# Reordering the opening attention of a fused attention and expert-mixture kernel: four scores in a row on two PSUM tiles, and a rearranged chunk 0

## The chip, the cores and the metric

The kernel runs on one core of one Trainium2 chip. The metric is device time in microseconds (us) of one execution; lower is better. The kernel before had a median of 497.34 us in its first 3 runs (496.2 to 497.48).

Names: PE is the matmul engine (TensorE), DVE the vector engine, ACT the scalar engine, POOL is GpSimd. PSUM is the memory that PE's results go to, cut in banks. Idle matmuls are matmuls of zeros whose results are not used. "The span" is the profiled execution, about 1.7 us shorter than its device time.

## The reference, cut to what matters

```python
# attention: batch 8, heads 8, sequence 576, head dimension 64
k_p = k.reshape(B, H, 72, 8, D).mean(axis=3)      # keys and values pooled by 8: 72 of each
v_p = v.reshape(B, H, 72, 8, D).mean(axis=3)
attn = softmax(q @ k_p.T / sqrt(D))               # (cut: written out in the original)
x = (attn @ v_p) reshaped to (4608 tokens, 512)
# four experts, every token through all of them
p = domain_probs / (domain_probs.sum(-1, keepdims=True) + 1e-9)
for e in range(4):
    out += p[:, e:e+1] * (maximum(x @ w1[e], 0) @ w2[e])     # w1: 512x1024, w2: 1024x512
```

## The kernel before

The kernel works in 9 chunks of 512 tokens: one for each batch's first 512 tokens, and a last one of the eight remainders. Three stages matter here.

1. **Batch 0's attention** (until about 25 us). Nothing else can fill PE yet. It runs pooling matmuls for keys and values, two groups of four heads by two halves of tokens = four "scores" (each 8 matmuls, then one exp on ACT), four contexts (one for each 128 tokens; matmuls, then a divide on DVE), a turn (transpose on PE, then a copy) of each context, and first-layer matmuls on 128 tokens at a time with the early half of w1 of expert 0.
2. **Chunk 0** (to about 69 us). The rest of the four experts for batch 0, with batch 1's attention woven in, as keys, values and weights land by DMA.
3. **The steady loop** (to the end). Both layers are multiplied as 2x2 blocks with seven products instead of eight, so sums of blocks (of x, of the weights, of the hidden layer) are formed on DVE first. The attention of the next batches is woven in; x of batch 2 and later is transposed by DMA.

The opening, as the kernel before has it (cuts are marked):

```python
    def two_banks(b):
        return att_first[turn_of("att", 2)] if b < 2 else att   # the two 2-bank tiles in turn

    def sum_keys(g):
        copies = (nc.vector.tensor_copy, nc.scalar.copy)
        for copy, (hs, kp) in zip(copies, sum_pool("kraw", g), strict=True):
            copy(out=kp_all[0:SP, hs], in_=kp.unsqueeze(2).to_broadcast([SP, 2, 2, D]))

    def context_half(r, g):
        # ... cut: x_tok is allocated ...
        c_ps = two_banks(0)                     # a whole 2-bank tile for half a context
        # ... cut: 4 matmuls, then divide() on DVE

    def scores_first(group, tok):
        # ... cut ...
        sc_ps = two_banks(0)[:].rearrange("p a (h n) -> p a h n", n=P)
        # ... cut: 8 matmuls, then one exp of 72x1024 on ACT

    def attention_first():
        # ... cut: queries, idle matmuls ...
        sum_keys(0)
        idle(1)
        keys(0, lo)
        sum_keys(1)
        scores_first(0, 0)
        keys(0, hi)
        sum_values(0)
        scores_first(1, 0)
        context_half(0, 0)
        sum_values(1)
        turn_half(0, 0)
        idle(1, chains[0][:])
        context_half(0, 1)
        scores_first(0, 1)
        idle(1, chains[1][:])
        turn_half(0, 1)
        context(0, 1)
        up_first(range(0, 4), first)
        turn(0, 1)
        scores_first(1, 1)                      # the fourth score, after first-layer work
        idle(1)
        up_first(range(0, 4), second)
        context(0, 2)
        context(0, 3)
        up_first(range(4, FCH), first)          # from here on the late half of w1
        turn(0, 2)
        up_first(range(4, 6), second)
        turn(0, 3)
        up_first(range(6, FCH), second)
        up(0, 0, range(FCH), half)
```

In chunk 0 the touched part is:

```python
        sums[1][3]()
        fold_keys(1, every)                     # DVE: adds up batch 1's keys, once they landed
        for i in range(3):
            up(0, 3, (i,))
            down(0, 0, 4 + i)
        queries(1, 0)
        # ... cut: queries, up(0, 3, ...), keys(1), scores(1, 0..2) ...
        fold_values(1, every)
        # ... cut: loads for batch 2 ...
        down_plain(0, 1, 0)
        scores(1, 3)
        down_plain(0, 1, 1)
        context(1, 0)
        # ... cut
```

```python
        POOLED = (4,)
        # ... cut
                down(*below_of[t2], i2, t2 % 2, POOLED)
```

The softmax here doesn't subtract the row's maximum and nothing guards it: scores larger than these inputs give would overflow.

## Time and profile before

| | kernel before |
|---|---|
| device time, median (range) of the first 3 runs | 497.34 us (496.2 to 497.48) |
| PE busy | 98% of the span, at a clock of 0.999 |
| first pooled-key matmul ("first key sum") | 7.92 us |
| expert 1's first 512-column first-layer matmul | 24.89 us |
| first matmul of the steady loop | 69.07 us |

The last three marks are read from the timeline. The document uses lengths made of them: **A**, from the first key sum to expert 1's first layer (16.97 us); **B**, from there to the steady loop (44.18); **C**, from there to the end of the span (425.1). A and B are what the change touches.

From the page of the kernel before: its span, busy times by engine, and the shares of the chain that ended last.

```profile
span 494.2 us, 11449 instructions
...
PE 486.7 (98%) x4656; PEld 405.9 (82%) x4663; DVE 375.9 (76%) x755; ACT 302.9 (61%) x562; POOL 115.8 (23%) x114
...
PE 98%; DVE 1%; issue 0%; DVEq 0%
```

PE is the limit, and the chain is PE almost without a break. A saved microsecond of PE waiting in A or B should therefore show at the end, if nothing later takes it back.

From the timeline of the kernel before, from 0 to 26 us. Columns: start, duration, engine, line, operation, output<-input by the program's names, shapes, count; in brackets the idle time before and what ended it.

```profile
1.26 5.20 PE L323 MATMUL unit<-H 128*128 128x512 bf16 x14 [1.26 <-DVE H L812]
...
7.92 0.69 PE L302 MATMUL unit<-wt_bf,S 64*72 64x128 bf16 x18
...
10.59 1.02 ACT L509 ACTIVATE expT<-att_first 72x1024 bf16<-72x1024 f32 x1
...
12.03 1.02 ACT L509 ACTIVATE expT<-att 72x1024 bf16<-72x1024 f32 x1 [0.42 <-PE att L505]
...
14.37 1.02 ACT L509 ACTIVATE expT<-att_first 72x1024 bf16<-72x1024 f32 x1 [0.85 <-PE att_first L505]
...
15.19 0.78 PE L592 MATMUL unit<-xT,w_bf 128*128 128x128 bf16 x8
...
16.70 0.40 PE L505 MATMUL att_first<-qT,kpT 64*128 64x128 bf16 x8
...
17.14 1.02 ACT L509 ACTIVATE expT<-att_first 72x1024 bf16<-72x1024 f32 x1 [0.31 <-PE att_first L505]
...
24.89 1.03 PE L577 MATMUL o_ps<-xT,w_bf 128*128 128x512 bf16 x3
```

The first line is the opening run of idle matmuls, the second the first key sum. The four ACT lines are the four exps. They start 2.67, 4.11, 6.45 and 9.22 us after the first key sum, though each takes only 1.02 us; three of them ended an idle spell of ACT that waited for PE's scores. The line at 16.70 is the fourth score, between first-layer matmuls that began at 15.19.

From the timeline of the kernel before, PE only, from 66 to 72 us, the first matmul of the steady loop:

```profile
69.07 0.60 PE L650 MATMUL unit<-xT,w_bf 128*128 128x256 bf16 x4
```

From the view of waits of the kernel before, PE only. Columns: who waited (engine, tile, line), for whom, us in total, times, longest.

```profile
PE unit L323 <- DVE kp L311: 0.5, 1, 0.5
PE o_ps L293 <- DVE kp L311: 0.4, 1, 0.4
PE o_ps L416 <- DVE x_tok L389: 0.3, 2, 0.2
PE att_first L401 <- DVE vp L316: 0.2, 1, 0.2
```

PE waits for the pooled keys (kp), the divided context (x_tok) and the pooled values (vp).

From the timeline of the kernel before, from 117 to 124 us, three of the sums on batch 2's x, and POOL's accumulating add:

```profile
120.91 0.43 DVE L238 TENSOR_TENSOR xs<-xs,xT 128x512 bf16<-128x512 bf16 x1 [0.89 <-DMA xT<-x_tok]
...
121.25 0.42 DVE L238 TENSOR_TENSOR xT<-xT 128x512 bf16<-128x512 bf16 x1
...
121.59 0.42 DVE L238 TENSOR_TENSOR xs<-xT,xs 128x512 bf16<-128x512 bf16 x1
121.75 1.40 POOL L732 TENSOR_TENSOR acc<-acc,addend 128x512 f32<-128x512 f32 x1
```

DVE waited for x to land by DMA, then ran its sums in 0.42 us each; POOL's add was issued 0.16 us after the last of them began.

### The profile page before, as it was taken

The numbers are of one execution on the slowest core, as the hardware profiler recorded it, in microseconds if no ns is written. First come the engines' busy times: TensorE is split into PE (matmuls) and PEld (weight loads), VectorE is DVE, ScalarE is ACT, GpSimd is POOL, SyncE is SP. The second block draws the span as 40 slices with busy tenths as digits, with TensorE's granted clock in tenths as the row PEclk, the third lists the DMA queues.
The fourth block names the chain that finished last, engine by engine and source line by source line (L and its number), as shares of the span: only waits on it lengthen the run. The fifth ranks groups of instructions, "written<-read, shape, count | busy, mean of one in ns | idle before, by whom it ended". The sixth has DMA issues, their size and how long they took to land.

```text
span 494.2 us, 11449 instructions
## 1 busy us (share of the span) xinstructions
PE 486.7 (98%) x4656; PEld 405.9 (82%) x4663; DVE 375.9 (76%) x755; ACT 302.9 (61%) x562; POOL 115.8 (23%) x114
## 2 busy tenths in 40 slices
PE   8999999999999999999999999999999999999996
PEld 4746468888889888888898889888888888888885
DVE  5495889799768975798669876796678766876674
ACT  4666536865775568656765676557655566556650
POOL 8320413233342154114421362111000100011010
PEclk9999999999999999999999999999999999999999
DMA  9999996997879669453975397320211010003003
GB/s 199 208 204 203 207 161 114 107 70 95 100 103 59 90 66 142 47 78 40 164 63 78 37 144 75 54 47 31 68 23 23 21 65 1 13 23 86 1 1 85
DMA packets 101811, 41.95 MB, mean 85 GB/s; under 512 B 73840, under 2 KB 100208, under 8 KB 101760
## 3 DMA queue, kind: packets, MB, share of 16 engines
q0 software_dynamic: 56928, 22.42, 40.8%
q1 hardware_dynamic: 43728, 17.77, 18.2%
q10 hardware_dynamic: 1104, 1.05, 0.6%
q8 instruction: 36, 0.59, 0.5%
q14 instruction: 15, 0.12, 0.1%
HBM read 45.69 MB, written 9.44 MB: 112 GB/s over the span
## 4 chain that ended last, share of the span: by engine, by line
PE 98%; DVE 1%; issue 0%; DVEq 0%
PE o_ps L718 41%; PE unit L650 40%; PE unit L577 4%; PE o_ps L744 3%; PE att L373 2%; PE att L425 2%; PE unit L323 1%; PE unit L776 1%; PE o_ps L577 1%; PE unit L592 0%; PE unit L302 0%; PE att L479 0%; PE att L462 0%; PE att_first L443 0%; PE o_ps L592 0%
## 5 line engine op out<-in xcount | busy, mean ns | idle before, releaser
L793 DVE SCALAR_TENSOR_TENSOR acc<-o_ps,p_all,acc 128x256 f32<-128x256 f32 (+1 forms) x285 | 127.2, 487 | 52.0 <-PE o_ps L718 34.6
L718 PEld LDWEIGHTS <-H 128*128 128x128 bf16 x1320 | 129.1, 98 | 16.2 <-issue 0.2
L650 PEld LDWEIGHTS <-w_bf 128*128 128x128 bf16 x1024 | 97.7, 98 | 15.1 <-issue 3.6
L631 DVE CUSTOM_DVE_ANT_0 H<-unit,partial 128x512 bf16<-128x512 f32 x128 | 87.5, 686 | 25.5 <-PE unit L650 20.9
L718 PE MATMUL o_ps<-w_bf,H 128*128 128x256 bf16 x792 | 102.6, 273 | 0.0
L650 PE MATMUL unit<-xT,w_bf 128*128 128x256 bf16 x672 | 96.4, 273 | 0.0
L665 ACT COPY partial<-unit 128x512 f32<-128x512 f32 x128 | 72.0, 590 | 33.2 <-PE unit L650 33.0
L732 POOL TENSOR_TENSOR acc<-acc,addend 128x512 f32<-128x512 f32 x24 | 30.5, 1271 | 253.7 <-ACT addend L730 197.8
L650 PEld LDWEIGHTS <-wu_bf 128*128 128x128 bf16 x768 | 73.3, 98 | 10.0 <-issue 1.5
L650 PE MATMUL unit<-xs,wu_bf 128*128 128x256 bf16 x512 | 76.9, 273 | 0.0
L718 PE MATMUL o_ps<-wt_bf,H 128*128 128x256 bf16 x528 | 68.4, 273 | 0.0
L718 PEld LDWEIGHTS <-S 128*128 128x128 bf16 x528 | 51.7, 98 | 6.4
L671 ACT ACTIVATE H<-unit 128x512 bf16<-128x512 f32 x64 | 38.2, 597 | 29.5 <-PE unit L650 29.3
L667 ACT ACTIVATE H<-unit 128x512 bf16<-128x512 f32 x64 | 38.8, 607 | 27.8 <-PE unit L650 27.8
L663 ACT COPY unit<-unit 128x512 f32<-128x512 f32 x64 | 37.4, 584 | 15.4 <-PE unit L650 15.4
L650 PE MATMUL unit<-xs,w_bf 128*128 128x256 bf16 x256 | 38.5, 273 | 0.0
L791 ACT ACTIVATE acc<-o_ps,p_all 128x256 f32<-128x256 f32 x72 | 30.2, 471 | 11.2 <-PE o_ps L718 9.9
L147 POOL DMA_DIRECT2D vraw<-in_v_dram x20 | 29.0, 1448 | 26.3 <-DMA vraw<-in_v_dram 19.8
L147 POOL DMA_DIRECT2D kraw<-in_k_dram x20 | 25.9, 1294 | 37.8 <-DMA kraw<-in_k_dram 37.8
L718 PE MATMUL o_ps<-w_bf,S 128*128 128x256 bf16 x264 | 34.2, 273 | 0.0
L718 PE MATMUL o_ps<-wt_bf,S 128*128 128x256 bf16 x264 | 34.2, 273 | 0.0
L650 PE MATMUL unit<-xT,wu_bf 128*128 128x256 bf16 x224 | 33.6, 272 | 0.0
(150 smaller groups left out, 514.3 us busy)
## 6 DMA issues: line engine op xcount, KB each, us to landing
out_dram<-acc SPq DMA_DIRECT2D x32, 256.0 KB, 4.2
w_bf<-in_moe_w_dram POOLq DMA_DIRECT2D x7, 1024.0 KB, 23.7
q_sb<-in_q_dram POOLq DMA_DIRECT2D x7, 512.0 KB, 9.7
vraw<-in_v_dram POOLq DMA_DIRECT2D x22, 144.0 KB, 6.7
kraw<-in_k_dram POOLq DMA_DIRECT2D x21, 144.0 KB, 5.5
w_bf<-in_moe_w_dram POOLq DMA_DIRECT2D x2, 512.0 KB, 8.1
wt_bf<-in_k_dram POOLq DMA_DIRECT2D x4, 144.0 KB, 5.5
wt_bf<-in_v_dram POOLq DMA_DIRECT2D x4, 144.0 KB, 4.2
```

Source lines behind the costliest of these rows:

```text
L147: nc.gpsimd.dma_start(out=raw[:], in_=rows_of(src, b, 2 * part, 2 * part + 2), accum_op=ALU.add if part else ALU.bypass)
L577: nc.tensor.matmul(out_ps, lhsT=w1_bf[:, e, kc, fc * P:(fc + 1) * P], rhs=xT[:, kc, at], start=(kc == 0), stop=(kc == KC - 1), skip_group_ ...
L631: nc.vector._custom_dve(TENSOR_ADD_SAT, out=dst, in0=ps, in1=part, s0=LARGEST, s1=0.0)
L650: nc.tensor.matmul(ps[:, n * HN:(n + 1) * HN], lhsT=lhs[:, kc, f:f + P], rhs=rhs[:, kc, :], start=(not grows and n == 0 and kc == 0), stop ...
L663: nc.scalar.copy(out=units[unit][1][:], in_=ps)
L665: nc.scalar.copy(out=part[:, step - 2], in_=ps)
L667: nc.scalar.activation(out=quarter(0, 0), in_=ps, func=ACT.Relu)
L671: nc.scalar.activation(out=quarter(0, 1), in_=ps, func=ACT.Relu)
L718: nc.tensor.matmul(ps[:, j], lhsT=lhs[:, i, j * P:(j + 1) * P], rhs=rhs[:, i, :], start=(not grows and i == 0 and j == 0), stop=(i == HF - 1),
L732: nc.gpsimd.tensor_add(out=dst, in0=dst, in1=addend[:])
L791: nc.scalar.activation(out=dst, in_=o_ps, func=ACT.Copy, scale=prob)
L793: nc.vector.scalar_tensor_tensor(out=dst, in0=o_ps, scalar=prob, in1=dst, op0=ALU.mult, op1=ALU.add,)
```

## The change

Its intent: let ACT run the four exps without gaps, so that everything behind the last one (contexts 2 and 3, their turns, the last first-layer blocks) is no longer held up. For this, the scores alternate between two 2-bank tiles, and the first context in two halves goes to the single banks that the second layer will use later. The order behind it changes: all first-layer work on the early half of w1, for all four token blocks, comes before any on the late half. Chunk 0 is reordered so that batch 1's keys and scores start earlier among other work, and the loads of expert 1's w2 and batch 1's values trade places.

The diff also moves some copies between DVE and ACT (of pooled keys and values, of the turn of context 1, and of batch 1's keys and queries).

The core of the diff (long parts cut):

```diff
-    def context_half(r, g):
+    def context_half(r, g, bank):
-        c_ps = two_banks(0)
+        c_ps = bank.rearrange("p (a n) -> p a n", a=1)
 # ... cut: scores_first, sum_keys, sum_values, turn_half and context also take their bank
-        sum_keys(0)
-        idle(1)
+        work, (B2, A2) = units[1], att_first
+        sum_keys(0, work)
+        idle(1, A2[:, 0])
+        sum_keys(1, [B2[:, 0], B2[:, 1]])
         keys(0, lo)
-        sum_keys(1)
-        scores_first(0, 0)
+        scores_first(0, 0, A2)
         keys(0, hi)
-        # ... cut: the old order, shown above
+        sum_values(0, work)
+        scores_first(1, 0, B2)
+        context_half(0, 0, chains[1][:])
+        scores_first(0, 1, A2)
+        sum_values(1, work)
+        turn_half(0, 0, chains[1][:])
+        scores_first(1, 1, B2)
+        context_half(0, 1, chains[0][:])
+        context(0, 1, A2)
+        idle(2, chains[1][:])
+        turn_half(0, 1, chains[0][:])
+        context(0, 2, B2)
+        idle(1, chains[1][:])
+        up_first(range(0, 2), first)
+        turn(0, 1)
+        up_first(range(2, 4), first)
+        context(0, 3, A2)
+        turn(0, 2)
+        up_first(range(0, 4), second)
+        turn(0, 3)
+        up_first(range(0, 4), third)
+        up_first(range(0, 4), fourth)
+        up_first(range(4, FCH), first)
+        up_first(range(4, FCH), second)
+        up(0, 0, range(4, FCH), half)
 # ... cut: chunk 0
         sums[1][3]()
-        fold_keys(1, every)
-        for i in range(3):
-            up(0, 3, (i,))
-            down(0, 0, 4 + i)
+        fold_keys(1)
+        up(0, 3, (0, 1))
+        down(0, 0, 4)
+        up(0, 3, (2, 3))
         queries(1, 0)
         queries(1, 1)
+        down(0, 0, 5)
+        keys(1, every)
 # ... cut: down(0, 0, ...) later, scores(1, ...) earlier, value fold in parts
 # ... cut: loads
         load_q(1)
+        load_w2(1)
         load_whole(1, v, "vraw")
-        load_w2(1)
```

More of the change, by code (lines that the diff above doesn't have):

```diff
@@ L257, in one_bank, with folds @@
         return spare_bank() if b == 0 else two_banks(b)[:, 0]
-    def fold(raw, hs):
-        nc.vector.tensor_add(out=raw[:, hs, 0:4, :], in0=raw[:, hs, 0:4, :],
-                             in1=raw[:, hs, 4:8, :])
-        nc.vector.tensor_add(out=raw[:, hs, 0:2, :], in0=raw[:, hs, 0:2, :],
-                             in1=raw[:, hs, 2:4, :])
+    def folds(raw):
+        return [lambda n=n: nc.vector.tensor_add(
+            out=raw[:, :, 0:n, :], in0=raw[:, :, 0:n, :], in1=raw[:, :, n:2 * n, :]) for n in (4, 2)]
     def fold_wide(what, part):
@@ L274, in fold_wide, with fold_keys @@
             nc.vector.tensor_add(out=raw[:], in0=raw[:], in1=a)
-    def fold_keys(b, hs):
+    def fold_keys(b):
         raw = raw_k if b >= BUSY else raws[("kraw", b)]
         if b < BUSY:
-            fold(raw, hs)
+            for do in folds(raw):
+                do()
         for dup in range(2):
-            nc.vector.tensor_add(out=kp_all[0:SP, hs, dup, :], in0=raw[:, hs, 0, :],
-                                 in1=raw[:, hs, 1, :])
+            nc.vector.tensor_add(out=kp_all[0:SP, :, dup, :], in0=raw[:, :, 0, :], in1=raw[:, :, 1, :])
     def keys(b, hs):
@@ L293, in keys, with sum_pool @@
             nc.tensor.transpose(kpt_ps[:, h, :], kp_all[0:SP, h], ident[:SP, :SP])
-        nc.vector.tensor_copy(out=state[("kpT", b)][:, hs, 0:SP], in_=kpt_ps[:, hs])
-    def sum_pool(nm, g):
+        copy = nc.scalar.copy if b else nc.vector.tensor_copy
+        copy(out=state[("kpT", b)][:, hs, 0:SP], in_=kpt_ps[:, hs])
+    def sum_pool(nm, g, banks):
         n = 2 * D
-        banks = [work_bank()[0:SP, 0:n] for _ in range(2)]
+        banks = [bank[0:SP, 0:n] for bank in banks]
         for r in range(ROWS):
@@ L306, in sum_pool, with sum_keys, sum_values @@
             yield slice(h, h + 2), banks[half].rearrange("j (h d) -> j h d", d=D)
-    def sum_keys(g):
-        copies = (nc.vector.tensor_copy, nc.scalar.copy)
-        for copy, (hs, kp) in zip(copies, sum_pool("kraw", g), strict=True):
+    def sum_keys(g, banks):
+        copies = (nc.scalar.copy if g else nc.vector.tensor_copy, nc.scalar.copy)
+        for copy, (hs, kp) in zip(copies, sum_pool("kraw", g, banks), strict=True):
             copy(out=kp_all[0:SP, hs], in_=kp.unsqueeze(2).to_broadcast([SP, 2, 2, D]))
-    def sum_values(g):
-        copies = (nc.vector.tensor_copy, nc.scalar.copy if g else nc.vector.tensor_copy)
-        for copy, (hs, vp) in zip(copies, sum_pool("vraw", g), strict=True):
-            copy(out=vps[0][:, hs, 0:D], in_=vp)
+    def sum_values(g, banks):
+        for hs, vp in sum_pool("vraw", g, banks):
+            nc.vector.tensor_copy(out=vps[0][:, hs, 0:D], in_=vp)
     def idle(n, w_ps=None):
@@ L325, in open_bank, with values_folds @@
     def open_bank(ps):
-        nc.tensor.matmul(ps, lhsT=ident[:], rhs=w2_bf[:, 0, 0, :], skip_group_check=True)
-    def fold_values(b, hs):
+        nc.tensor.matmul(ps, lhsT=ident[:], rhs=w1_bf[:, 0, 0, 0:NT], skip_group_check=True)
+    def values_folds(b):
         raw = raw_v if b >= BUSY else raws[("vraw", b)]
-        if b < BUSY:
-            fold(raw, hs)
-        nc.vector.tensor_add(
-            out=vps[b % 3][:, hs, 0:D], in0=raw[:, hs, 0, :], in1=raw[:, hs, 1, :]
-        )
+        return (folds(raw) if b < BUSY else []) + [lambda: nc.vector.tensor_add(
+            out=vps[b % 3][:, :, 0:D], in0=raw[:, :, 0, :], in1=raw[:, :, 1, :])]
     def queries(b, pair=0):
@@ L355, in queries @@
                 )
-        copy = nc.scalar.copy if b == 0 and pair % 2 else nc.vector.tensor_copy
+        copy = nc.scalar.copy if pair in ((1, 3), (1, 2))[b] else nc.vector.tensor_copy
         copy(out=state[("qT", b)][:, 2 * pair:2 * pair + 2], in_=qt_ps)
@@ L405, in context_half, with turn_half @@
             )
-        divide(c_ps[:, 0:1], state[("x", 0, r)][:, g:g + 1])
-    def turn_half(r, g):
+        divide(c_ps, state[("x", 0, r)][:, g:g + 1])
+    def turn_half(r, g, bank):
         if ("xT", 0) not in state:
@@ L412, in turn_half @@
         ks = slice(g * HK, (g + 1) * HK)
-        xt_ps = chains[1 - g][:].bitcast(BF16)[:, 0:HK * P].rearrange("p (k t) -> p k t", t=P)
+        xt_ps = bank.bitcast(BF16)[:, 0:HK * P].rearrange("p (k t) -> p k t", t=P)
         for i in range(HK):
@@ L417, in turn_half, with context @@
         nc.vector.tensor_copy(out=state[("xT", 0)][:, ks, r * P:(r + 1) * P], in_=xt_ps)
-    def context(b, r):
+    def context(b, r, c_ps=None):
         expT, vp = state[("expT", b)], vps[b % 3]
         x_tok = npool.tile([P, 2, NPAIR, D], BF16, name="x_tok", bufs=4)
-        c_ps = two_banks(b)
+        if c_ps is None:
+            c_ps = two_banks(b)
         for h in range(H):
@@ L440, in turn @@
             return
-        xt_ps = (one_bank(b) if b else att_first[1][:, 0] if r == 3 else chains[0][:]).bitcast(BF16)[:, 0:KC * P].rearrange("p (k t) -> p k t", t=P)
+        xt_ps = (units[1][0][:] if b else att_first[1][:, 0] if r == 3 else chains[0][:]).bitcast(BF16)[:, 0:KC * P].rearrange("p (k t) -> p k t", t=P)
         for kc in range(KC):
             nc.tensor.transpose(xt_ps[:, kc, :], x_tok[:, kc * P:(kc + 1) * P], ident[:])
-        copy = nc.vector.tensor_copy if b == 0 and r % 2 else nc.scalar.copy
+        copy = nc.vector.tensor_copy if b == 0 and r == 3 else nc.scalar.copy
         copy(out=dst, in_=xt_ps)
@@ L491, in rem_turn, with scores_first @@
         )
-    def scores_first(group, tok):
+    def scores_first(group, tok, sc_ps):
         qT = state[("qT", 0)]
@@ L499, in scores_first @@
         hs = groups(0)[group]
-        sc_ps = two_banks(0)[:].rearrange("p a (h n) -> p a h n", n=P)
+        sc_ps = sc_ps[:].rearrange("p a (h n) -> p a h n", n=P)
         for hh in range(H // 2):
@@ L516, in attention_first @@
         lo, hi = groups(0)
-        first, second, half = slice(0, P), slice(P, 2 * P), slice(HN, NT)
+        first, second, third, fourth = (slice(r * P, (r + 1) * P) for r in range(NR))
+        half = slice(HN, NT)
         idle(14)
@@ L528, in attention_first @@
         idle(1)
-        sum_keys(0)
-        idle(1)
+        work, (B2, A2) = units[1], att_first
+        work = [work[0][:], work[1][:]]
+        sum_keys(0, work)
+        idle(1, A2[:, 0])
+        sum_keys(1, [B2[:, 0], B2[:, 1]])
         keys(0, lo)
-        sum_keys(1)
-        scores_first(0, 0)
+        scores_first(0, 0, A2)
         keys(0, hi)
-        sum_values(0)
-        scores_first(1, 0)
-        context_half(0, 0)
-        sum_values(1)
-        turn_half(0, 0)
-        idle(1, chains[0][:])
-        context_half(0, 1)
-        scores_first(0, 1)
+        sum_values(0, work)
[10 more added lines that the diff above has]
+        context(0, 2, B2)
         idle(1, chains[1][:])
-        turn_half(0, 1)
-        context(0, 1)
-        up_first(range(0, 4), first)
+        up_first(range(0, 2), first)
         turn(0, 1)
-        scores_first(1, 1)
-        idle(1)
+        up_first(range(2, 4), first)
+        context(0, 3, A2)
+        turn(0, 2)
         up_first(range(0, 4), second)
-        context(0, 2)
-        context(0, 3)
+        turn(0, 3)
+        up_first(range(0, 4), third)
+        up_first(range(0, 4), fourth)
         up_first(range(4, FCH), first)
-        turn(0, 2)
-        up_first(range(4, 6), second)
-        turn(0, 3)
-        up_first(range(6, FCH), second)
-        up(0, 0, range(FCH), half)
+        up_first(range(4, FCH), second)
+        up(0, 0, range(4, FCH), half)
     hidden = {(0, 0): H_bufs[0], (0, 1): H_bufs[1], (0, 2): H_third, (0, 3): H_bufs[0]}
@@ L737, in down, with down_plain @@
             store(c, row, cols)
-    def down_plain(c, e, r):
+    def down_plain(c, e, r, fcs=range(FCH)):
         H_sb = hidden[(c, e)]
         o_ps = chains[r % 2][:]
-        for fc in range(FCH):
+        for fc in fcs:
             lhs = H_sb[:, fc // HF, r // 2, fc % HF, (r % 2) * P:(r % 2 + 1) * P]
@@ L747, in down_plain @@
             )
-        add(o_ps, c, e, r, slice(0, DM), True)
+        if fcs.stop == FCH:
+            add(o_ps, c, e, r, slice(0, DM), True)
     room = wu_bf[:, 0, 0].rearrange("p k (i d) -> p (k i) d", d=HD)
@@ L838, in first_chunk @@
                 sums[2][i]()
-            if i == 3:
+            if i == 4:
                 open_bank(chains[1][:])
                 each(*weight_sums(0))
-            if i >= 4:
-                down(0, 0, i - 4)
-                if i in (5, 6):
-                    hidden_sums(0, 0, i - 3)
+            if i == 5:
+                down(0, 0, 0)
+                hidden_sums(0, 0, 2)
+            if i == 6:
+                down(0, 0, 1)
+                hidden_sums(0, 0, 3)
+                down(0, 0, 2)
+        down(0, 0, 3)
         sums[1][3]()
-        fold_keys(1, every)
-        for i in range(3):
-            up(0, 3, (i,))
-            down(0, 0, 4 + i)
+        fold_keys(1)
+        up(0, 3, (0, 1))
+        down(0, 0, 4)
+        up(0, 3, (2, 3))
         queries(1, 0)
         queries(1, 1)
-        up(0, 3, (3,))
+        down(0, 0, 5)
+        keys(1, every)
         queries(1, 2)
+        down(0, 0, 6)
+        scores(1, 0)
+        queries(1, 3)
+        turn_of("att", 2)
         up(0, 3, (4,))
-        queries(1, 3)
-        keys(1, every)
         each(*sums[3][0:3])
+        scores(1, 1)
         up(0, 3, (5,))
-        scores(1, 0)
+        scores(1, 2)
         up(0, 3, (6,))
-        scores(1, 1)
+        each(*weight_sums(1)[0:3])
+        scores(1, 3)
         up(0, 3, (7,))
-        scores(1, 2)
-        fold_values(1, every)
+        fold_first, *fold_rest = values_folds(1)
+        fold_first()
+        down_plain(0, 1, 0)
+        each(*fold_rest)
         load_wide(0, 0)
@@ L873, in first_chunk @@
         load_wide(1, 2)
-        each(*weight_sums(1)[0:1])
-        down_plain(0, 1, 0)
-        scores(1, 3)
-        each(*weight_sums(1)[1:2])
         down_plain(0, 1, 1)
+        down_plain(0, 1, 2, range(0, 3))
         context(1, 0)
-        down_plain(0, 1, 2)
+        down_plain(0, 1, 2, range(3, FCH))
         context(1, 1)
@@ L888, in first_chunk @@
         turn(1, 2)
-        each(*weight_sums(1)[2:3])
         down_plain(0, 2, 1)
@@ L930, in pieces_later @@
                 put(start + plan["queries"], lambda b=b: queries(b))
-                put(start + plan["keys"], lambda b=b: fold_keys(b, every))
+                put(start + plan["keys"], lambda b=b: fold_keys(b))
                 put(start + plan["keys"] + (b > BUSY), lambda b=b: keys(b, every))
-                put(start + plan["values"], lambda b=b: fold_values(b, every))
+                put(start + plan["values"], *values_folds(b))
                 put_each("scores", [lambda b=b, pair=pair: scores(b, pair) for pair in range(NPAIR)])
```

## The prediction

> **What bounds the kernel now.** TensorE. The page shows PE busy 486.7 of 494.2 us (98%), clock 0.999, and the chain that ended last is 98% PE. [...] I count issue intervals: in the timeline 128-column matmuls follow one another every 56 ns, 256-column ones every 109, 512-column ones every 216. PE is full from 66 us on (table of windows). All that the change touches lies before the steady loop (its first matmul at 69.1 us); what is saved there passes to the end one for one.
>
> **Where PE loses time there.**
> - Attention of batch 0, from the first pooled-key matmul (7.92 us) to the half-wide first layer (21.39): 13.5 us. Its matmuls need about 9.4 at their issue intervals, the idle matmuls 1.1. Some 3 us are waits: for kp, vp, x_tok, and the copy behind turn 3.
> - 21.39 to 51.4 us: none (group starts match the sums of intervals to 0.1).
> - 51.4 to 68.9 us: about 0.4, 0.1 at each score group.
>
> **What the change does.** PE work is nearly unchanged: the order of instructions shows 16 more matmuls, since half of the 256-column first-layer ones become 128-column ones (32 x 56 for 16 x 109 ns: +0.05 us). Idle matmuls: 21 in both. The four exps (1.02 us each on ACT, starting at 10.59, 12.03, 14.37, 17.14) come back to back, about 10.4, 11.5, 12.5, 13.5. Contexts 2 and 3 no longer wait for the last one, and four blocks of first-layer work on the early half of w1 precede the first need of its second half (landing near 18.4). Against this, DVE becomes the chain between 12 and 18 us: vp casts (0.28 each), half divides (0.18+0.42) and three whole ones (0.21+0.69), with the second half-turn's copy behind a whole divide. First-layer work starts near 15.8 us, later than before's 15.19, but then runs without waits; expert 1's first layer starts near 23.9 instead of 24.89. Gain about 1.0 us.
>
> **A floor by DMA.** Expert 1's w1 lands near 23.3 us (issue near 9.4, 13.6 to landing; POOL's next wait on that semaphore ends at 23.42, though the view of waits names ACT). So this stage can't gain over 1.6. Later landings fit: w2 of expert 0 33.7, keys of batch 1 42.2, queries 44.8. Swapping values and w2 of expert 1 (landing 48.5 and 53.7 in before) brings w2 to about 50 and values to 53.6; the new order needs them near 50 and 57.
>
> Second stage: scores beside query transposes, key wait (0.1) hidden: gain 0.2 to 0.4 us, at risk of a wait of some tenths for queries, keys or vp.
>
> **Sum:** -1.0 -0.3 = -1.3 us (0.3%): 496.0 us, range 494.6 to 497.3. Chances: faster 0.01, same 0.98, slower 0.01.
>
> **What would show it.** Four exps without gaps between 10.4 and 14.6; expert 1's first 128x512 matmul at 23.3 to 24.2; PE waits for x_tok/xT from 13 to 15.8 larger than before, none from 18 to 23; the steady loop starting at 67.3 to 68.2; the rest as long as before.
>
> **What would make it wrong.** A later landing of either weight of expert 1; DVE's order delaying the first half-turn until the gain is gone; kpT's copy on ACT behind relus, starving batch 1's scores; later loads for batch 2 (they wait for the last value fold) opening a hole after 70 us; or the spread of runs (496.2 to 497.5), as large as the gain.

## The result

| | before | after |
|---|---|---|
| device time, median of 6 runs (range) | 496.46 us (495.67 to 497.48) | 495.36 us (494.6 to 496.83) |
| profiled execution: device time, span | 495.89, 494.2 us | 496.83, 495.1 us |
| A | 16.97 us | 15.83 us |
| B | 44.18 us | 44.18 us |
| C | 425.1 us | 426.7 us |
| X | 52.9 us | 54.9 us |

The ratio is 0.9978, with a 95% interval of 0.9959 to 0.9996. Ratios here are computed as the mean time of one kernel's fast runs over that of the other's of the same rounds, so they are not quite the ratio of the medians quoted. The changed kernel is 1.1 us faster by medians, 0.2%: the same, at 2%.

The profiled execution is the slowest of the changed kernel's six, and its span is longer than the one of before. This has to be explained beside the gain.

From the page of the changed kernel:

```profile
span 495.1 us, 11473 instructions
...
PE 486.8 (98%) x4672; PEld 406.2 (82%) x4679; DVE 375.7 (76%) x751; ACT 305.0 (62%) x566; POOL 115.8 (23%) x114
...
PE 95%; DVE 2%; DMA 1%; issue 1%; DVEq 0%
```

PE's busy time is that of before; the chain is no longer 98% PE: DVE has 2% and DMA 1% of it.

From the timeline of the changed kernel, from 0 to 26 us, with the columns as before:

```profile
1.26 5.70 PE L322 MATMUL unit<-H 128*128 128x512 bf16 x14 [1.26 <-DVE H L814]
...
8.43 0.69 PE L302 MATMUL unit<-wt_bf,S 64*72 64x128 bf16 x18
...
11.14 1.02 ACT L506 ACTIVATE expT<-att_first 72x1024 bf16<-72x1024 f32 x1 [0.40 <-PE att_first L502]
...
12.25 1.02 ACT L506 ACTIVATE expT<-att 72x1024 bf16<-72x1024 f32 x1
...
13.17 1.01 ACT L506 ACTIVATE expT<-att_first 72x1024 bf16<-72x1024 f32 x1
...
13.74 0.40 PE L502 MATMUL att<-qT,kpT 64*128 64x128 bf16 x8
...
14.18 1.02 ACT L506 ACTIVATE expT<-att 72x1024 bf16<-72x1024 f32 x1
...
16.16 0.49 PE L593 MATMUL unit<-xT,w_bf 128*128 128x128 bf16 x6 [0.16 <-DVE xT L413]
...
24.26 1.03 PE L578 MATMUL o_ps<-xT,w_bf 128*128 128x512 bf16 x3
```

The exps now start 2.71, 3.82, 4.74 and 5.75 us after the first key sum: ACT is busy from 11.14 to 15.20 almost without a gap. The fourth score runs at 13.74, ahead of all first-layer work. First-layer work begins at 15.73 (a group not shown) and after a wait again at 16.16, so no earlier than before, measured from the first key sum (7.30 against 7.27 us); it is what follows that is shorter. The first line is not the change's doing: the same 14 idle matmuls took 5.70 us in this execution and 5.20 in that of before, and all that follows is half a microsecond later.

The end of B, from the timeline of the changed kernel, PE only, from 66 to 72 us; 68.44 less 24.26 is 44.18, as before:

```profile
68.44 0.60 PE L651 MATMUL unit<-xT,w_bf 128*128 128x256 bf16 x4
```

From the view of waits of the changed kernel, PE only:

```profile
PE unit L651 <- DVE H L632: 1.3, 1, 1.3
...
PE att_first L502 <- DVE kpT L294: 0.4, 1, 0.4
PE o_ps L412 <- DVE x_tok L385: 0.3, 1, 0.3
PE unit L593 <- DVE xT L413: 0.2, 1, 0.2
```

The last three lines stand against the four of before: 0.9 us of named waits in A instead of 1.4. The rest of the gain is in gaps that this view doesn't name. Taking the distance between the starts of successive matmuls and subtracting what one issues in (216, 109 and 57 ns for 512, 256 and 128 columns; 28 for those on 64 rows, which start in pairs, and 33 for those on 72), and adding up what is left where it exceeds 40 ns, A has 4.23 us of such gaps before and 3.09 after. The difference, 1.14 us, is the whole change of A; what is left for the matmul work itself is equal, 12.74 us in both.

The first line of the waits is new, lies outside A and B, and is as large as the gain (by the distances between matmul starts, 1.49 us). From the timeline of the changed kernel, from 117 to 124 us:

```profile
120.89 0.42 DVE L238 TENSOR_TENSOR xs<-xs,xT 128x512 bf16<-128x512 bf16 x1 [1.50 <-DMA xT<-x_tok]
...
121.12 1.57 POOL L733 TENSOR_TENSOR acc<-acc,addend 128x512 f32<-128x512 f32 x1
121.23 1.75 DVE L238 TENSOR_TENSOR xT<-xT 128x512 bf16<-128x512 bf16 x1
...
122.91 0.41 DVE L238 TENSOR_TENSOR xs<-xT,xs 128x512 bf16<-128x512 bf16 x1
```

x of batch 2 lands at the same time as in the profile of before, but the loop had begun 0.6 us earlier, and POOL's add is now ahead of DVE's second sum. That sum takes 1.75 us where it took 0.42, the last sum ends late, and PE waits 1.3 us at 124 us for what DVE does next. The add was issued 0.11 us ahead of the sum, and the sum ended 0.29 us after the add did. In the kernel before it was the other way round: the add was issued 0.16 us behind a sum, the sum took its 0.42 us, and the add took 1.40. The traces of the experiments below agree: with this one, in four traces a sum issued 0.11 to 0.50 us behind this add took 1.03 to 1.75 us and ended 0.28 to 0.30 us after it. The add took 1.40 to 1.57 us in the four traces in which a sum was still running when it was issued, and 1.25 to 1.26 in the seven others that have it. By what means the one holds up the other is not shown.

So four questions were put to the chip. The letters are those of the expectations below; where a text uses another, it says there what it means.
- Is the gain made in the attention (A), and by what: the early fourth score (A1) or the new order of the first-layer blocks (A2)?
- Do chunk 0's order and the swapped loads gain anything, or are they only needed to keep the gain (E, for the swap)?
- Is the wait at 124 us made by the collision of POOL's add with DVE's sum (C), or by the lateness of x as such (D)?
- Can the wait be taken away, and does a version then beat both?

### The profile page after: what moved, and what is told of

The parts are those of the page before. It is cut to its first block, busy times and chain, and to the rows that moved or that the text cites. A ratio compares the mean times of both kernels' runs of the same rounds, so it can differ in the third digit from the quotient of the medians.

```text
span 495.1 us, 11473 instructions
## 1 busy us (share of the span) xinstructions
PE 486.8 (98%) x4672; PEld 406.2 (82%) x4679; DVE 375.7 (76%) x751; ACT 305.0 (62%) x566; POOL 115.8 (23%) x114
## 4 chain that ended last, share of the span: by engine, by line
PE 95%; DVE 2%; DMA 1%; issue 1%; DVEq 0%
PE o_ps L719 40%; PE unit L651 39%; PE unit L578 4%; PE o_ps L745 3%; PE att L369 2%; PE att L422 1%; PE unit L322 1%; PE unit L778 1%; DMA xT<-x_tok 1%; PE unit L593 1%; PE o_ps L578 1%; DVE acc L795 1%; PE unit L302 0%; PE o_ps L593 0%; PE att L476 0%
## 5 line engine op out<-in xcount | busy, mean ns | idle before, releaser
L795 DVE SCALAR_TENSOR_TENSOR acc<-o_ps,p_all,acc 128x256 f32<-128x256 f32 (+1 forms) x285 | 127.0, 485 | 52.3 <-PE o_ps L719 34.0
L664 ACT COPY unit<-unit 128x512 f32<-128x512 f32 x64 | 37.4, 584 | 16.8 <-PE unit L651 16.8
```

Of the source, the lines that this page charges most:

```text
L664: nc.scalar.copy(out=units[unit][1][:], in_=ps)
L795: nc.vector.scalar_tensor_tensor(out=dst, in0=o_ps, scalar=prob, in1=dst, op0=ALU.mult, op1=ALU.add,)
```

## The experiments

All results were correct, and all executions had a granted clock of 0.998 to 1.0. Lengths are from the profiled execution; they are compared by stages, since the time of the first key sum varies (7.62 to 8.52 us) without a cause in the kernels. The runs were made in batches on two chips; each time with several runs is compared with the kernel before in the same batch, on the same chip.

### The changed kernel once more, and the kernel before once more

No edit.

> The changed kernel, not altered, for a second trace and tighter times. Theory A (the gain is made in the attention stage alone): from the first query transpose to expert 1's first 512-column matmul about 17.5 us (18.6 in before), from there to the steady loop's first matmul 44.2 us as in before; time 1.0 to 1.3 us under before. Theory B (the stall of 1.5 us at 124 us in the first trace is a standing cost of the change): it is there again, and the loop to the end again takes 426.5 us. Theory C (it comes of a chance overlap of a GpSimd add with a DVE operation on x): here the loop takes about 425.1 us and the DVE operation about 0.42 us and not 1.75.

> Before, not altered, for a second trace: attention stage 18.6 us, 44.2 us to the loop, 425.1 us from there; the first query transpose may start some tenths away from 6.29 us if the start of PE's full rate wanders between runs (6.29 and 6.79 us in the two traces so far).

The changed kernel: 495.35 us median of 6 runs (494.67 to 496.84) against 496.42 of before (11 runs), ratio 0.998 (0.9964 to 0.9996). A 15.84, B 44.20, C 426.8. The profiled execution was again the slowest, 496.84 us, and had a stretched sum again: this time the last of the three, 1.49 us, behind an add issued at 121.47. That is what theory B of the text above expected (a standing cost), and not what theory C did; only the third trace, below, speaks against theory B. By the distances between matmul starts PE's wait at 124 us is 1.11 us here, and C holds another one, 0.60 us at 81.7, for queries of the remainders that land by DMA. The kernel before in one look: 496.32 us, A 16.97, B 44.18, C 425.7; the 0.6 us of C over 425.1 are mostly a wait for an exp at 94.2 us.

A repeats to 0.01 us in both kernels, and so does the gain. Of the changed kernel's 12 runs in the two batches 9 lie between 494.60 and 495.71, the two profiled ones at 496.83 and 496.84, and one at 496.13. That the nine lack the wait at 124 us follows from their times only; no trace of them exists.

### The attention alone

The new attention with the old chunk 0 and the old order of loads.

```diff
 # against the changed kernel
-        (chunk 0, folds, copies of keys and queries as changed)
+        (chunk 0, folds, copies of keys and queries as in the kernel before)
         attention_first()
+        turn_of("att", 2)        # so that batch 1 meets the two tiles in the old turn
-        load_w2(1)
         load_whole(1, v, "vraw")
+        load_w2(1)
```

> Before with the changed attention of batch 0 (scores back to back, contexts in chain banks, first-layer blocks reordered), but the old order of chunk 0 and of the loads. Theory A: attention stage 17.5 us as in the whole change; but w2 of expert 1 lands near 53.7 us, and down_plain of expert 1 now wants it near 53.2, so PE waits 0.3 to 0.6 us there, stage to the loop 44.5 to 44.8; gain in all 0.5 to 0.8 us. Rival (the reorder of chunk 0 and the load swap do nothing): 44.2 us, gain 1.1 us.

Measured: 495.61 us median of 6 runs (495.26 to 499.42), ratio 1.0002 (0.9976 to 1.0028; two of the six, 497.07 and 499.42, lift the mean). A 15.89, B 45.05, C 425.1.

The gain of A is there in full without chunk 0's new order, and 0.87 us of it is then given back in B. I had expected a wait for expert 1's w2. It was another one. From the timeline of this kernel, from 41 to 48 us:

```profile
42.79 1.22 DVE L262 TENSOR_TENSOR wt_bf<-wt_bf 72x2048 bf16<-72x2048 bf16 x1 [3.61 <-DMA wt_bf<-in_k_dram]
...
45.45 1.65 DVE L797 SCALAR_TENSOR_TENSOR acc<-o_ps,p_all,acc 128x256 f32<-128x256 f32 x4
...
46.37 1.03 PE L722 MATMUL o_ps<-wt_bf,H 128*128 128x256 bf16 x8 [0.70 <-DVE acc L797]
```

DVE stood idle for 3.61 us until batch 1's keys landed at 42.79, then folded them, and only then reached the four accumulations that free the second layer's banks; PE waited for these at 46.37. DVE took its work here in the order of the program, the fold at 42.79 and the accumulations at 45.45: a fold placed where its keys had just landed in the old timing held up what stood behind it (PE by 0.70 us at 46.37) when PE came a microsecond earlier. The 0.87 us are not the change's alone: this execution began early (first key sum at 7.74 us, against 8.43 in the changed kernel's profile) and expert 1 at 23.63 instead of 24.26, while the keys landed at nearly the same time (42.8 and 42.6). At the start of the changed kernel's profile some 0.2 us would be left, by an estimate from these times. The two combined versions below start expert 1 earlier still (23.39 and 23.37) and have B of 44.19 and 44.22, so the new chunk 0 does take the wait away.

### Chunk 0 alone

The old attention with the new chunk 0 and the swapped loads.

```diff
 # against the changed kernel
-        (attention_first and its helpers as changed)
+        (attention_first and its helpers as in the kernel before)
         attention_first()
+        turn_of("att", 2)
```

> The changed kernel with the old attention of batch 0. Theory A: attention stage 18.6 us, then 44.2 us to the loop: same time as before within 0.2 us. Prediction's term (reorder of chunk 0 worth 0.2 to 0.4 us by itself): 43.8 to 44.0 us.

Measured: 496.25 us median of 6 runs (496.12 to 498.05), ratio 1.0001 (0.9985 to 1.0016). A 16.97, B 44.18, C 425.1.

Chunk 0's order gains nothing by itself: B is equal to 0.01 us. My prediction had counted 0.2 to 0.4 us for it.

### The fourth score late again

The new tiles and banks, but the fourth score behind first-layer work, and the tail of the attention in the order of before.

```diff
         turn_half(0, 0, chains[1][:])
-        scores_first(1, 1, B2)
         context_half(0, 1, chains[0][:])
 # ... cut
         up_first(range(2, 4), first)
+        scores_first(1, 1, B2)
         up_first(range(0, 4), second)
 # ... cut: contexts 2 and 3 and the late half of w1 as in the kernel before
```

> The changed kernel, but the fourth score after the first first-layer block, as before, with contexts 2 and 3 and the first-layer groups behind it in the old order. Theory A1: three scores early keep part of the gain; the fourth exp starts 2 to 3 us later, and turns 2 and 3 wait as in before: stage 17.9 to 18.3 us. Rival (the gain is only the new banks and the work overlapped before the first exp): 17.5 us.

Measured in one look: 498.47 us; A 16.95, B 44.18, C 427.1 (a sum was stretched to 1.03 us, and 0.55 us are a wait for an exp at 94.8). From the first query transpose to expert 1's first layer it took 18.59 us, more than I had expected; the changed kernel took 17.47, that of before 18.60. From the timeline of this kernel, the third and fourth exps:

```profile
13.20 1.01 ACT L506 ACTIVATE expT<-att_first 72x1024 bf16<-72x1024 f32 x1
...
17.74 1.02 ACT L506 ACTIVATE expT<-att 72x1024 bf16<-72x1024 f32 x1
```

The third exp is as early as in the changed kernel, the fourth is 9.28 us after the first key sum, and all of the gain is gone. By the count of gaps used above this kernel has 4.20 us of them in A. In the first 4.7 us after the first key sum it is equal to the changed kernel (1.84 us, where before had 2.20); what it lost lies behind that, 2.37 us of gaps against 1.26. So the two tiles and the key sums, with the copies moved there, were worth about 0.4 us by themselves, and the early fourth score decides whether that and the rest are kept.

### The old order of the first-layer blocks

```diff
         turn(0, 3)
-        up_first(range(0, 4), third)
-        up_first(range(0, 4), fourth)
         up_first(range(4, FCH), first)
         up_first(range(4, FCH), second)
-        up(0, 0, range(4, FCH), half)
+        up(0, 0, range(FCH), half)
```

> The changed kernel, but the first layer of expert 0 in the old order after turn 3: the first two token blocks on the late half of w1, then the half-wide groups for all of F. Theory A1 (the stage gains in front, by the scores and contexts being early): attention stage 17.4 to 17.6 us as in the change. Rival A2 (it gains by putting four blocks of first-layer work before the late half of w1): 17.9 us or more, with PE waits between 18.5 and 22.5 us.

Measured in one look: 495.55 us; A 15.79, B 44.18, C 425.3. From the first query transpose: 17.42 us.

A is as short as in the changed kernel. That the early half's blocks of all tokens come before the late half of w1 is worth nothing here, so A2 falls. Its C is short, but it is one execution.

### The swapped loads undone

```diff
-        load_w2(1)
         load_whole(1, v, "vraw")
+        load_w2(1)
```

> The changed kernel with the old order of loads (values of batch 1 before w2 of expert 1). Theory E (the swap is what lets the new order of chunk 0 run without waits): w2 lands near 53.7 us, DVE's sums of it, which stand near 50 us in its program, wait 3 us or more, the value fold behind them ends near 59 us, and PE waits 0.3 to 0.8 us before batch 1's first context: 44.5 to 45.0 us from expert 1's first matmul to the loop. Rival (the swap does nothing): 44.2 us.

Measured in one look: 497.3 us; A 15.83, B 44.80, C 426.6 (with a sum of 1.72 us). From the timeline of this kernel, from 52 to 60 us:

```profile
53.73 0.69 DVE L238 TENSOR_TENSOR wt_bf<-w_bf 128x1024 bf16<-128x1024 bf16 x1 [1.65 <-DMA w_bf<-in_moe_w_dram]
...
58.30 0.42 DVE L330 TENSOR_TENSOR vp<-wt_bf 72x512 bf16<-72x512 bf16 x1
...
58.79 0.43 PE L422 MATMUL att_first<-vp,expT 72*128 72x65 bf16 x8 [0.25 <-DVE vp L330]
```

DVE waits 1.65 us for expert 1's w2, does its sums at 53.73, reaches the last fold of the values at 58.30, and PE's context waits for that fold at 58.79. B is 0.62 us longer than in the changed kernel. The swap is needed to keep the gain, as E said.

### The key fold moved behind three second-layer steps

The attention alone, with DVE's key fold later.

```diff
 # against the attention alone
         sums[1][3]()
-        fold_keys(1, every)
         for i in range(3):
             up(0, 3, (i,))
             down(0, 0, 4 + i)
+        fold_keys(1, every)
         queries(1, 0)
```

> The kernel attn_only (new attention, old chunk 0, old loads) with the key fold of batch 1 moved behind the last three second-layer steps of expert 0, so that their adds on DVE don't wait for the keys' landing (42.8 us). Expected: the wait of 0.87 us at 46.4 us is gone; but then expert 1's second layer wants its w2 29.5 us after expert 1's first matmul, and w2 lands near 53.8 us: a wait of 53.8 minus that time, 0.6 us if expert 1 begins at 23.6 us, none if it begins at 24.3. Rival (the 0.87 us had another cause): the wait stays.

Measured in one look: 496.04 us; A 16.28 (it waited for key data that landed no earlier, after an early start), B 45.25, C 425.1. From the timeline of this kernel, from 45 to 50 us:

```profile
45.96 1.21 DVE L262 TENSOR_TENSOR wt_bf<-wt_bf 72x2048 bf16<-72x2048 bf16 x1
...
48.61 0.41 DVE L356 COPY qT<-att 128x512 bf16<-128x512 bf16 x1
...
49.08 0.38 PE L352 MATMUL att<-ident,q_sb 128*128 128x128 bf16 x4 [0.90 <-DVE qT L356]
```

The wait at 46.37 is gone, and a new one stands at 49.08: the copies of the transposed queries are now behind the fold on DVE, and PE waits 0.90 us for one of them. B is not shorter but 0.20 us longer. I had meant to see whether a wait for w2 would appear behind the first one; since the wait only moved, this run says nothing on that. It does confirm that the place of the fold in DVE's order is what matters in the attention-alone kernel.

### Without POOL's add where batch 2's x lands

```diff
-                down(*below_of[t2], i2, t2 % 2, POOLED)
+                down(*below_of[t2], i2, t2 % 2, POOLED if t2 != 3 else ())
```

> The changed kernel with the one GpSimd add that overlapped the sums of batch 2's x (fourth iteration of the loop) done by DVE instead. Theory C (the stall of 1.1 to 1.5 us near 124 us in both traces of the changed kernel is a DVE operation on x that lasts 1.5 to 1.75 us instead of 0.42 while GpSimd adds): no such stretch even where x lands at 120.9 us, loop to the end 425.1 to 425.4 us, no time near 496.8 among the runs, median 0.1 to 0.5 us under the changed kernel's. Rival D (x of batch 2 landing late is enough for the stall): still 426 us or more where x lands at 120.9 us.

Measured: 495.32 us median of 5 runs (494.68 to 495.81) against 496.59 of before, ratio 0.9969 (0.9942 to 0.9995). A 15.83, B 44.19, C 425.7, X 53.0. No sum was stretched. The 0.6 us of C over 425.1 are three small waits that the kernel before has not: 0.37 at 124.1, 0.15 at 126.9 and 0.16 at 135.7.

The profiled execution is 1.0 us shorter than the changed kernel's two, as the collision (C) asks. But the case that the text names, x landing at 120.9, did not arise: DVE began its sums at 120.32, and x had landed 51.8 us after the loop's start, against 52.3 and 52.7 in the changed kernel's two traces. So this run does not decide between C and D. The median is not better than the changed kernel's 495.36: most executions have nothing to gain from this.

### The changed kernel a third time

No edit.

> The changed kernel once more, for a third trace. From the first key sum to expert 1's first 512-column matmul 15.83 us, then 44.2 us. If x of batch 2 lands by 120.0 us, the loop takes 425.1 to 425.4 us and there is no stall near 124 us; if it lands near 121 us the x sums meet the GpSimd add and the loop takes over 426 us (as in both traces so far).

Measured in one look: 496.32 us; A 17.19, B 44.18, C 425.1, X 52.6. From the timeline of this kernel, from 117 to 124 us:

```profile
121.02 0.42 DVE L238 TENSOR_TENSOR xs<-xs,xT 128x512 bf16<-128x512 bf16 x1 [0.60 <-DMA xT<-x_tok]
...
121.36 0.42 DVE L238 TENSOR_TENSOR xT<-xT 128x512 bf16<-128x512 bf16 x1
...
122.14 1.26 POOL L733 TENSOR_TENSOR acc<-acc,addend 128x512 f32<-128x512 f32 x1 [0.63 <-DVE xs L238]
```

This time x landed at 121.02 but the add came at 122.14, behind the sums; no sum was stretched, and C is short. So the same kernel has both cases, and which comes first, the add or the sum, separates them. The expectation had gone by the time of landing as such, and missed; what counts is its distance from the loop's start, which came late here, at 69.47: 51.4 us. The long A has another cause, from the view of waits of this kernel:

```profile
PE unit L302 <- DMA wt_bf<-in_v_dram: 1.2, 1, 1.2
```

PE waited 1.2 us for the pooled values' data, the last part of which landed at 13.9 us in this execution, and at 11.6 to 12.6 in the 13 other traces; the loads before it came as usual. Without that wait A would be about 16.0. That the start depends on when the loads land is one more source of spread of about a microsecond.

### Two combined versions

The first has no POOL add there, no idle matmul between the key sums, and the second half-turn's copy on ACT. The second keeps the idle matmul.

```diff
 # first
-        nc.vector.tensor_copy(out=state[("xT", 0)][:, ks, r * P:(r + 1) * P], in_=xt_ps)
+        copy = nc.scalar.copy if g else nc.vector.tensor_copy
+        copy(out=state[("xT", 0)][:, ks, r * P:(r + 1) * P], in_=xt_ps)
 # ... cut
         sum_keys(0, work)
-        idle(1, A2[:, 0])
 # ... cut
-                down(*below_of[t2], i2, t2 % 2, POOLED)
+                down(*below_of[t2], i2, t2 % 2, POOLED if t2 != 3 else ())
 # second: the same with idle(1, A2[:, 0]) in its place
```

> The changed kernel with three edits: the second half-turn's copy on ACT (idle there) instead of behind a whole divide on DVE; the idle matmul between the two key sums taken out, so that the first key transpose comes earlier; and the GpSimd add of no_pool_add. Expected: first-layer work starts 0.3 us earlier by each of the first two, stage 16.8 to 17.0 us; but expert 1's first matmul not before its w1 lands (23.4 to 23.7 us in all traces), so that an early start gains less. Time 0.3 to 0.7 us under the changed kernel's median.

> The changed kernel with two of best1's edits: the second half-turn's copy on ACT, and no GpSimd add in the loop's fourth iteration; the idle matmul stays. If the ACT copy is what best1 gained by (0.31 us from the first key sum on): 15.5 us from the first key sum to expert 1's first 512-column matmul, as in best1. Time 0.2 to 0.5 us under the changed kernel's median of 495.35, and all fast runs under 496.3.

The first: 495.12 us median of 6 runs (494.57 to 500.16), ratio 0.9983 (0.9947 to 1.0019; without the one of 500.16 they end at 495.74). A 15.52, B 44.19, C 425.3. The copy on ACT starts at 14.87, while DVE's whole divide, behind which it used to wait, runs from 14.64 to 15.33; A is 0.31 us shorter. The second: 495.29 us median of 6 (494.64 to 496.85), ratio 0.9978 (0.9962 to 0.9994). A 15.75, of which some 0.2 are a wait for key data, B 44.22, C 427.5.

Neither clearly beats the changed kernel (495.36 and 495.35), so the 0.3 to 0.7 and 0.2 to 0.5 us expected were missed; so was the stage of the first (17.26 us from the first query transpose, not 16.8 to 17.0; it, too, waited some 0.2 us for key data), and one fast run of the second, the profiled one, is over 496.3. In both, expert 1's first layer starts at 23.39 and 23.37 us. By the record of the loads its weights had landed at 22.8 in both, and PE did not wait for them: the floor by DMA of the prediction was near, but no run shows that it held.

The second one has more to say on the wait at 124 us. From its timeline, from 117 to 124 us:

```profile
121.39 0.43 DVE L238 TENSOR_TENSOR xs<-xs,xT 128x512 bf16<-128x512 bf16 x1 [2.85 <-DMA xT<-x_tok]
...
121.73 0.42 DVE L238 TENSOR_TENSOR xT<-xT 128x512 bf16<-128x512 bf16 x1
```

Here POOL has no add, the sums take their usual 0.43 and 0.42 us, and yet X is 54.9 and C 427.5: x landed so late, 53.7 us after the loop's start, that PE waited all the same. So lateness alone (D) is sufficient, in this one trace. Over all 14 traces one rule holds: where the last sum of batch 2's x ends at most 53.0 us after the loop's start, C is 425.1 to 425.7; where it ends 54.8 us or more after it, C is 426.6 to 427.5. The landing alone separates the same traces: at most 51.8 us after the loop's start, or at least 52.3.

How much of the wait is the collision's (C) can be estimated. In the five traces with the wait, X less PE's wait at 123 to 126 us (and less PE's earlier waits in the loop) is 53.3 to 53.4 us, so any later end of the sums seems to be paid in full. Without its stretch of 1.33 us the sums of the changed kernel's first trace would have ended near 53.5, so some 1.3 of its 1.5 us are the stretch; in its second trace (a stretch of 1.07) it is all 1.1. No run with x as late as there and no add tests this.

All runs in one table (us):

| kernel | median, runs | A | B | C | X |
|---|---|---|---|---|---|
| before | 496.46, 6 | 16.97 | 44.18 | 425.1 | 52.9 |
| before, again | 496.32, 1 | 16.97 | 44.18 | 425.7 | 52.6 |
| after | 495.36, 6 | 15.83 | 44.18 | 426.7 | 54.9 |
| after, again | 495.35, 6 | 15.84 | 44.20 | 426.8 | 55.0 |
| after, third | 496.32, 1 | 17.19 | 44.18 | 425.1 | 52.6 |
| attention alone | 495.61, 6 | 15.89 | 45.05 | 425.1 | 52.0 |
| chunk 0 alone | 496.25, 6 | 16.97 | 44.18 | 425.1 | 52.0 |
| fourth score late | 498.47, 1 | 16.95 | 44.18 | 427.1 | 55.3 |
| old block order | 495.55, 1 | 15.79 | 44.18 | 425.3 | 52.2 |
| loads not swapped | 497.3, 1 | 15.83 | 44.80 | 426.6 | 54.8 |
| key fold later | 496.04, 1 | 16.28 | 45.25 | 425.1 | 52.0 |
| no POOL add | 495.32, 5 | 15.83 | 44.19 | 425.7 | 53.0 |
| combined, first | 495.12, 6 | 15.52 | 44.19 | 425.3 | 52.6 |
| combined, second | 495.29, 6 | 15.75 | 44.22 | 427.5 | 54.9 |

## Why the prediction was right, and where it was not

The time predicted was 496.0 us, from 494.6 to 497.3; measured were 495.36, and 1.1 us gained against 1.3 predicted. That the sums agree so well is partly luck: the attention gained 0.14 us more than was said and chunk 0 none of its 0.3, and the prediction started from 497.34 us, a median of three runs that came down by 0.9 us with three more. Point by point:

- **"Gain about 1.0 us" in the attention: right.** A lost 1.14 us and repeated to 0.01. Exps without gaps "between 10.4 and 14.6" came at 11.14 to 15.20: the same series, half a microsecond later through the longer opening. Expert 1 began at 24.26, predicted "23.3 to 24.2"; without that half microsecond it would have been 23.8. For the same reason, and for the term below, the loop began at 68.44, predicted "67.3 to 68.2". That first-layer work starts no earlier came as said, and so did its running without waits from 18 us on (before that, PE had gaps of 0.32 us at 16.16 and 0.18 at 17.61), and moving the fourth score back cost the whole gain.
- **The block order on the early half of w1, given as part of the reason: wrong.** Undoing it left A at 15.79.
- **"Second stage: ... gain 0.2 to 0.4 us", in the sum as -0.3: wrong; this is the term that was mis-sized.** It measured 0.00: B is 44.18 in both kernels, and also with chunk 0's order alone. I had read 0.1 us at each score group as waits that other work could hide. They are gaps at each switch of PE between 64-row score matmuls and 128-row ones: 95 to 96 ns on the way into a score group and 92 to 93 on the way out, in both kernels. Each kernel has eight such switches in B, 0.75 us in all, and no other gap over 40 ns but those where single matmul records seem to be missing from the trace; the predicted wait for keys is in neither. These gaps come with a switch, and with no wait in the profile, and they stayed when other work was put around them; what PE does in them is not shown. Fewer switches might save some of it, which no run tried. What chunk 0's order and the swapped loads do is keep the gain: with both undone 0.87 us came back as waits (in an execution that began early, see above), and with the swap undone 0.62.
- **The landings: right.** w2 of expert 1 was predicted near 50 us and landed at 50.3; the values were predicted at 53.6 and landed at 54.2.
- **"The rest as long as before": wrong for the profiled executions.** C was 1.6 and 1.7 us longer in two of three traces of the changed kernel (0.6 of the second at another place). The named risk, "a hole after 70 us" through later loads for batch 2, is near it, but the cause seen was another: x of batch 2, transposed by DMA, landed late by the loop's clock, and POOL's add, coming ahead of DVE's sum, stretched it. That the loop began earlier is not enough to explain it: the two combined versions began it at 67.58 and 67.59 us, and only one of them has the wait; and the kernel with the late fourth score began it last of all, at 69.59, and has it too.

What stays open: what decides when batch 2's x lands. In the nine traces in which DVE waited for it, it was complete between 119.1 and 123.2 us. The loop itself issues these transposes: the first came 34.95 to 35.56 us after its start in all 14 traces, but the fourth 47.1 to 48.8, and that one took 2.4 to 5.2 us to land (3.5 to 5.2 in the nine). With the old chunk 0 none of 4 traces had the late case, with the new one 5 of 10; loads for batch 2 begin at 58.3 us in the changed kernel and at 55.9 before. This is too few to say that the change makes it likelier, and no run tested the loads' start by itself.

The spread between profiled executions has one more source: the first query transpose came at 5.94 to 6.89 us over the 14 traces, with PE's first matmul at the same 1.26, because PE reached its full rate at different times: the idle matmuls at the start followed one another every 427 ns and then every 216, and the change came between 4.2 and 6.6 us, a range of 2.4 us. What decides when it comes is not shown. The first 14 idle matmuls so took 4.62 to 5.79 us, a range of 1.17; the query transposes vary by less, 0.95 us, since PE had to wait for the queries where it was fast early (0.16 us in the kernel with the key fold later, whose 14 took the 4.62). So the gain was compared by lengths between marks, not by spans.

## What to carry to other kernels

Where PE has no other work yet, as in an opening attention, what counts is when the last of a series of exps is ready: put the last score early, even if it delays the first of the work behind (here A was 15.83 us with the fourth score early, 16.95 with it late). When one stage got shorter here, loads that were under way (batch 1's keys landed at 42.2 us before and at 42.8 with the attention alone) and the order within each engine stayed as they were; so re-place every instruction whose data comes by DMA (a fold, a weight sum, a load's place in its queue), or the gain comes back as a wait further on (here 0.87 us with the old chunk 0 and the old loads, 0.62 with the old loads alone). And before counting a small gap as something to hide, see whether it comes with every switch of its kind (here 92 to 96 ns at each of eight).
